# Eight partitions 16 apart instead of 4 apart as the target of each exchange transfer in a gated FFT mix

## The chip, the cores and the metric

The kernel runs on one core of one Trainium2 chip. The metric is the device time of one execution in microseconds. Before the change three executions took 117.07, 117.38 and 120.54 us; the median is 117.38 us.

## What is computed

Two global spectral filters A and B are applied to the same input `x` of 2048 rows by 1024 columns in bf16, and a gate per row mixes them:

```python
X = jnp.fft.rfft2(x.astype(jnp.float32), axes=(-2, -1))
a = jnp.fft.irfft2(X * (A_w_r + 1j * A_w_i), s=(2048, 1024), axes=(-2, -1))
b = jnp.fft.irfft2(X * (B_w_r + 1j * B_w_i), s=(2048, 1024), axes=(-2, -1))
g = sigmoid((x * gate_w).sum(-1, keepdims=True))
out = g * a + (1 - g) * b
```

`A_x` is the `x` of both filters; the weights have 2048 by 513 entries each.

## The kernel before, in words

The row transform of length 2048 is split as 128 times 16. `f1` and `f1j` (L240 to L260) multiply the 16 slabs of x by a constant of 128 columns and leave, for 16 groups `t` of row frequencies, sums in the tile `y`. From there the work is done in 16 units `n`: eight for the even column frequencies (`par` 0) and eight for the odd ones (`par` 1). A unit holds two groups, `t = 2 u + tt` with `u = n % 8` and `tt` 0 or 1. Per unit:

- `f2` (L323) transforms along the columns on TensorE, `tc_` (L336) evicts to bf16 on ScalarE.
- `f3` (L341) does the rest of the row transform, 16 points with twiddles; `xc` (L366) evicts it.
- `cmul` (L382) multiplies by the weights of both filters on VectorE (two instructions, L388). The weights come from HBM, one load of about 0.5 MB per unit, issued on SyncE's queue by `load_w` (L189). Units 0 to 6 are loaded ahead; the later loads are issued inside the unit loop as buffers come free.
- `i1` (L395) adds the products and does the 16-point part of the inverse, for `r` = 0 and 1, 32 matmuls each (L404). `rlc` (L407) evicts each half into the tile `rl`, on ScalarE (L417) or VectorE (L415). `rl` has four buffers (`tag="rl", bufs=4`), so unit n+4 writes the buffer that unit n's transfers read.
- `ex` (L419) is the exchange. It moves `rl` to `RR[par]`, which is the tile `re` for the even units and `ro` for the odd ones, with two DMA transfers issued on GpSimd's queue (L424), one for each `tt`.

The exchange turns the layout around. Row `16 k + s1` of `rl` (k from 0 to 7) belongs to piece k of the group and to slab s1 of the output. A transfer takes the 128 rows of one `tt`, 2 KB each, and writes them to eight partitions, one for each k, in each of them 16 slots of 2 KB, one for each s1. That is 256 KB per transfer, 32 transfers in all. When all eight units of one parity have landed, all 128 partitions of `RR[par]` are filled, and `i2` (L428) contracts over the partitions, slab by slab, with the gated cosines and sines EA and EB as the moving operand. EA and EB are made by `gate_weights` (L312) from the gate and the constant `Ec`, whose row p must hold the wave of the group and piece that lies in partition p; this is the constant "E" (L75). The order of the partitions in `RR` is otherwise free, as `i2` sums over all of them.

After that come the inverse along the columns (`i3e`, `i3q`, `i3o`, `of`), the sums and differences of the halves (`ec`, `eq`, `eg`, `oc`, `fin`), some of them on GpSimd, and eight stores (`st`, and `oc_split` for the last).

The order of all instructions is written out by hand from L577 on. In the loop at L596 the step n holds f2, tc_ of unit n, f3, xc of unit n-1, i1r (i1, rlc and ex) of unit n-3 and the products of unit n-1. The last exchanges are `i1r(14)` and `i1r(15)` (L647, L648). Between them and the first use of `ro`, `op2(0)` at L665, stand the even half's `ep2` and `i3q` work (L649 to L664), which needs only `re`. TensorE takes its work in this order, and what is behind a waiting instruction waits too.

Of the kernel before, what the change touches and what calls it, by code (L numbers as in the profile page):

```python
# [28 lines left out]
def _bf16np(a):  # L29
    return np.ascontiguousarray(np.asarray(a, dtype=np.float32).astype(ml_dtypes.bfloat16))  # L30


def quad_reps(t):
    return (0, 32, 16, 48) if t == 0 else (t, t + 32, t + 64, t + 96)
# [9 lines left out]
def half_rows(t, jh):  # L44
    return np.array([k2 + 128 * k1 for k2 in half_k2(t, jh) for k1 in range(16)])
# [7 lines left out]
def make_constants():  # L53
    c = {}
    s2 = np.arange(128)
    F = np.zeros((128, NT, 2, 2, 2))
    E = np.zeros((NT, 2, 2, 2, 128))
    EZ = np.zeros((NT, 2, 2, 2, 128))
    for t in range(NT):
        for j, k2 in enumerate(quad_reps(t)):  # L60
            th = 2 * np.pi * s2 * k2 / 128
            F[:, t, j // 2, 0, j % 2] = np.cos(th)
            F[:, t, j // 2, 1, j % 2] = -np.sin(th)
            E[t, j // 2, 0, j % 2] = np.cos(th)
            E[t, j // 2, 1, j % 2] = np.sin(th)
            EZ[t, j // 2, 0, j % 2] = 2 * np.cos(th)
            EZ[t, j // 2, 1, j % 2] = -2 * np.sin(th)
            if k2 == 0:
                F[:, t, j // 2, 1, j % 2] = np.cos(np.pi * s2)
                E[t, j // 2, 1, j % 2] = np.cos(np.pi * s2)  # L70
                EZ[t, j // 2, 0, j % 2] = 1
                EZ[t, j // 2, 1, j % 2] = np.cos(np.pi * s2)
    F = F.reshape(128, 128)
    c["F1"] = _bf16np(np.concatenate([F, -F], axis=1))
    c["E"] = _bf16np(E.reshape(2, 4, 2, 8, 128).transpose(2, 0, 3, 1, 4).reshape(128, 128))  # L75
    c["EZ"] = _bf16np(EZ.reshape(128, 128) / 128)
    d = np.arange(256) + 0.5
    i = np.arange(256)
    FD = np.zeros((256, 2, 2, 256))
    dq = DD + 0.5  # L80
    IGE = np.zeros((2, 256, 256))
    IGO = np.zeros((2, 256, 512))
    do = np.concatenate([dq, 512 - dq])
    for eo in range(2):
        m = 2 * i + eo
        FD[:, eo, 0] = np.cos(2 * np.pi * np.outer(d, m) / D)
        if eo == 0:
            IGE[0] = 2 * np.cos(2 * np.pi * np.outer(m, dq) / D)
            IGE[0, 0] = 1
        else:  # L90
            IGO[0] = 2 * np.cos(2 * np.pi * np.outer(m, do) / D)
        m = 2 * i + (2 if eo == 0 else 1)
        FD[:, eo, 1] = -np.sin(2 * np.pi * np.outer(d, m) / D)
        if eo == 0:
            IGE[1] = -2 * np.sin(2 * np.pi * np.outer(m, dq) / D)
            IGE[1, 255] /= 2
        else:
            IGO[1] = -2 * np.sin(2 * np.pi * np.outer(m, do) / D)
    c["FD"] = _bf16np(FD.reshape(2, 128, 2, 2, 256).transpose(1, 2, 3, 0, 4))
    IGE = IGE[:, MSPLIT]  # L100
    c["IGE"] = _bf16np(IGE.reshape(4, 128, 256).transpose(1, 0, 2) / (S * D))
    c["IGO"] = _bf16np(IGO.reshape(4, 128, 512).transpose(1, 0, 2) / (S * D))
    s1 = np.arange(NS1)
    WF = np.zeros((128, NT, 3, 64))
    WI = np.zeros((128, NT, 4, 64))
    for t in range(NT):
        for jh in range(2):
            k = half_rows(t, jh)
            reps = quad_reps(t)[2 * jh:2 * jh + 2]
            al = np.zeros((NS1, 2, 2, 64), dtype=complex)  # L110
            be = np.zeros((2, 2, NS1, 64), dtype=complex)
            for p in range(64):
                w = np.exp(-2j * np.pi * k[p] * s1 / S)
                kk = k[p] % 128
                if kk in (0, 64):
                    cc = 0 if kk == 0 else 1
                    al[:, cc, 0, p] = w
                    be[cc, 0, :, p] = w.conj()
                    continue
                eps = 1 if kk in reps else -1  # L120
                j = reps.index(kk if eps > 0 else 128 - kk)
                al[:, 0, j, p] = w
                al[:, 1, j, p] = 1j * eps * w
                be[0, j, :, p] = w.conj()
                be[1, j, :, p] = 1j * eps * w.conj()
            al = al.reshape(64, 64)
            be = be.reshape(64, 64).T
            h = slice(64 * jh, 64 * jh + 64)
            WF[h, t, 0], WF[h, t, 1], WF[h, t, 2] = al.real, al.imag, -al.imag
            h = h if t % 2 == 0 else slice(64 - 64 * jh, 128 - 64 * jh)  # L130
            WI[h, t, 0], WI[h, t, 1], WI[h, t, 2], WI[h, t, 3] = be.real, be.imag, -be.imag, -be.real
    c["WF"] = _bf16np(WF)
    c["WI"] = _bf16np(WI)
    return c
# [3 lines left out]
def gated_mix(ctx, tc, x_in, we_in, wo_in, gw_in, out):  # L138
    nc = tc.nc
    cn = make_constants()  # L140
    dr = {n: nc.inline_tensor(a, name=f"cst_{n.lower()}").ap() for n, a in cn.items()}
    xv = x_in.flatten_outer_dims()
# [146 lines left out]
    RR = [r[:].rearrange("p (s f) -> p s f", s=NS1) for r in (Re, Ro)]  # L289
# [129 lines left out]
    def ex(n):  # L419
        u, par = n % NU, n // NU  # L420
        rl = RLs.pop(n)
        for tt in range(2):
            p0 = 64 * tt + 32 * (u // 4) + u % 4
            nc.gpsimd.dma_start(RR[par][p0:p0 + 29:4, :, :], rl[:, tt].rearrange("p r m -> p (r m)"))  # L424

    Vs, NV = {}, []

# [73 lines left out]
    def i1r(n, e0, e1):  # L501
        i1(n, 0)
        rlc(n, 0, e0)
        i1(n, 1)
        rlc(n, 1, e1)
        ex(n)
# [245 lines left out]
```

## Time and profile before

| what | us |
|---|---|
| three executions | 117.07, 117.38, 120.54 (median 117.38) |
| the profiled execution, its own time | 117.96 |
| its span | 116.1 |
| TensorE busy | 106.8 (92%) |
| VectorE busy | 95.0 (82%) |
| ScalarE busy | 85.9 (74%) |
| GpSimd busy | 64.5 (56%) |

The profiled execution is 0.58 us above the median; 1.86 us of its time lie outside the span. The mean granted TensorE clock was 0.98. The profile's page gives, for 40 equal slices of the span (2.90 us each), the busy tenths of each engine, the mean busy share of the 16 DMA engines and the GB/s that they moved. The view of groups shows for each line the number of instructions, the mean duration and the idle time of the engine just before them. "To landing" is the time from the issue of a transfer to the last semaphore update that tells of its arrival.

### The profile page before, as it was taken

What the parts mean: (1) busy time and instruction counts of PE and PEld (TensorE: products, weight loads), DVE (VectorE), ACT (ScalarE), POOL (GpSimd) and SP (SyncE); (2) the same over time, 40 slices, a digit from 0 to 9 for tenths busy, and PEclk for the clock granted to TensorE, in tenths of its full rate; (3) what the DMA queues carried; (4) which work ended last, traced back from release to release, by engine and by line L of the source; (5) the groups of instructions that cost most, each with busy time, mean ns of one, the idle gap of its engine ahead of it and who ended that gap; (6) DMA issues with size and microseconds to landing.
All of it is one profiled execution on the core that took longest, in us unless ns stands there. A gap on an engine that the chain in (4) does not pass through costs nothing.

```text
span 116.1 us, 3591 instructions
## 1 busy us (share of the span) xinstructions
PE 106.8 (92%) x1510; PEld 73.3 (63%) x1510; DVE 95.0 (82%) x124; ACT 85.9 (74%) x100; POOL 64.5 (56%) x83
## 2 busy tenths in 40 slices
PE   5999998999999999999999999999997999999900
PEld 2587797855565666555557655659986996677300
DVE  0048799597769999899989999998999779978960
ACT  4078867796998889889899999999756964564300
POOL 1379999902044414244433134446959399999670
PEclk9999999999999999999999999999999999999985
DMA  3999999999999999999999996577840000179684
GB/s 97 329 394 421 363 379 402 418 417 384 397 257 268 228 284 253 287 270 246 251 242 261 270 256 170 147 178 208 211 147 6 0 6 0 51 311 356 251 320 163
DMA packets 11567, 28.73 MB, mean 247 GB/s; under 512 B 3740, under 2 KB 4256, under 8 KB 11552
## 3 DMA queue, kind: packets, MB, share of 16 engines
q1 hardware_dynamic: 6624, 20.02, 47.9%
q0 software_dynamic: 4640, 8.41, 29.4%
q8 instruction: 12, 0.20, 0.7%
q10 hardware_dynamic: 288, 0.07, 0.3%
q14 instruction: 3, 0.02, 0.1%
HBM read 15.89 MB, written 4.19 MB: 173 GB/s over the span
## 4 chain that ended last, share of the span: by engine, by line
PE 51%; POOL 15%; DVE 10%; DMA 9%; issue 6%; ACT 5%; POOLq 1%; ACTq 0%; DVEq 0%
PE pt L404 19%; PE pt L331 9%; PE pt L259 9%; DMA ro<-rl 6%; POOL ot L531 6%; POOL ot L530 6%; DVE y L268 4%; PE pt L354 4%; DMA f<-cst_f 3%; DVE p L388 3%; POOL re L490 2%; DVE rl L415 2%; PE pv L354 2%; PE pv L436 2%; ACT rl L417 2%
## 5 line engine op out<-in xcount | busy, mean ns | idle before, releaser
L404 PE MATMUL pt<-p,wi 64*64 64x512 bf16 x464 | 28.0, 377 | 0.3 <-DVE rl L415 0.3
L388 DVE TENSOR_TENSOR p<-X,w 128x2048 bf16<-128x2048 bf16 (+1 forms) x22 | 25.7, 1224 | 0.1
L404 PEld LDWEIGHTS <-wi 64*64 64x64 bf16 x512 | 15.2, 106 | 9.8 <-issue 0.7
L417 ACT CAST rl<-pt 128x1024 bf16<-128x1024 f32 x21 | 21.4, 1062 | 0.0
L424 POOL DMA_DIRECT2D re<-rl x16 | 9.5, 600 | 19.4 <-issue 5.0
L338 ACT CAST T<-pt 128x1024 bf16<-128x1024 f32 x15 | 15.4, 1026 | 4.1 <-PE pt L331 4.0
L424 POOL DMA_DIRECT2D ro<-rl x16 | 9.5, 598 | 14.1 <-ACT rl L417 9.1
L331 PE MATMUL pt<-fd,y 128*128 128x256 bf16 x120 | 15.9, 274 | 0.6 <-DVE y L268 0.6
L331 PEld LDWEIGHTS <-y 128*128 128x128 bf16 x128 | 11.2, 98 | 7.0 <-issue 4.6
L268 POOL TENSOR_TENSOR y<-ro 128x256 bf16<-128x256 f32 x20 | 13.8, 733 | 0.7 <-ACT ro L285 0.7
L268 DVE TENSOR_TENSOR y<-pt,ro 128x256 bf16<-128x256 f32 x20 | 7.6, 420 | 7.5 <-ACT ro L285 6.9
L376 ACT CAST X<-pt 128x1024 bf16<-128x1024 f32 x12 | 12.6, 1048 | 0.2 <-PE pl L363 0.2
L490 POOL TENSOR_TENSOR re<-w 128x512 f32<-128x512 f32 x8 | 10.2, 1300 | 3.2 <-DVE w L484 1.9
L285 ACT COPY ro<-pt 128x768 f32<-128x768 f32 x10 | 8.0, 799 | 4.3 <-PE pt L259 3.7
L448 ACT CAST V<-pt 128x1024 bf16<-128x1024 f32 x9 | 8.9, 1018 | 2.8 <-PE pt L436 2.8
L415 DVE CAST rl<-pt 128x1024 bf16<-128x1024 f32 x8 | 9.8, 1222 | 1.1 <-PE pt L404 0.9
L259 PE MATMUL pt<-f,re 128*128 128x256 bf16 x80 | 10.5, 295 | 0.1
L259 PEld LDWEIGHTS <-re 128*128 128x128 bf16 x80 | 8.2, 106 | 3.1 <-DMA re<-in_x_dram 1.2
L436 PEld LDWEIGHTS <-ro 128*128 128x128 bf16 x128 | 7.6, 98 | 1.0 <-DMA ro<-rl 0.9
L436 PEld LDWEIGHTS <-re 128*128 128x128 bf16 x128 | 7.4, 98 | 0.7 <-issue 0.4
L354 PE MATMUL pt<-T,wf 64*64 64x512 bf16 (+2 forms) x144 | 7.5, 312 | 0.2 <-ACT T L338 0.2
L354 PEld LDWEIGHTS <-wf 64*64 64x64 bf16 x192 | 4.4, 105 | 5.0 <-issue 3.1
(90 smaller groups left out, 180.5 us busy)
## 6 DMA issues: line engine op xcount, KB each, us to landing
re<-rl POOLq DMA_DIRECT2D x16, 256.0 KB, 8.7
ro<-rl POOLq DMA_DIRECT2D x16, 256.0 KB, 5.5
out_dram<-ot SPq DMA_DIRECT2D x7, 512.0 KB, 3.3
re<-in_x_dram SPq DMA_DIRECT2D x6, 512.0 KB, 7.9
w<-in_wo_dram SPq DMA_DIRECT2D x6, 512.0 KB, 8.0
w<-in_we_dram SPq DMA_DIRECT2D x5, 516.0 KB, 9.0
eab<-in_we_dram SPq DMA_DIRECT2D x3, 516.0 KB, 11.0
re<-in_x_dram SPq DMA_DIRECT2D x4, 256.0 KB, 3.7
```

What stands on the lines that cost most here:

```text
L259: nc.tensor.matmul(o, lhsT=x[:, s1, h * 512 + q * 128:h * 512 + (q + 1) * 128], rhs=(bc(F1[:, 0, :]).to_broadcast([P, 2, 128]) if h == 0 e ...
L268: eng.tensor_tensor(o, i0, i1_, op)
L331: nc.tensor.matmul(ps[:, tt * 512 + r * 256:tt * 512 + r * 256 + 256], lhsT=y[:, par, e, q, 2 * t:2 * t + 2, :, :].rearrange("p j s c -> p ...
L338: nc.scalar.copy(out=T[:].rearrange("p a b -> p (a b)"), in_=PS.pop(("f2", n))[:])
L354: nc.tensor.matmul(ps[ho, tt * 512 + dst:tt * 512 + dst + ln], lhsT=WF[hp(jh), 2 * u + tt, w, :], rhs=T[hp(jh), tt, src:src + ln], start=( ...
L376: nc.scalar.copy(out=xo, in_=ps[:].rearrange("p (t r m) -> p t r m", t=2, r=2))
L388: nc.vector.tensor_tensor(p[:, :, :, 0:M], xb, Ws[n][:, :, :, 0:M], ALU.mult)
L404: nc.tensor.matmul(ps[hp(jh), tt * 512:(tt + 1) * 512], lhsT=WI[hin, 2 * u + tt, w, :], rhs=p[hin, tt, ri::2, o:o + 256], start=(k == 0), ...
L417: nc.scalar.copy(out=o_, in_=i_)
L424: nc.gpsimd.dma_start(RR[par][p0:p0 + 29:4, :, :], rl[:, tt].rearrange("p r m -> p (r m)"))
L436: nc.tensor.matmul(ps[:, s * 512 + ch * 128:s * 512 + ch * 128 + 128], lhsT=RR[par][:, s1, c0 + 256 * ab:c0 + 256 * ab + 128], rhs=Ew[:, s ...
L490: eng.tensor_tensor(o, ls[:, 0], ls[:, 1], op)
```

## The change

Each exchange transfer still writes eight partitions with 16 slots of 2 KB. Before, the partitions were 4 apart, all in one block of 32 partitions: transfer `tt` of unit `u` wrote 64 tt + 32 (u // 4) + u % 4 + 4 k. After, they are 16 apart and lie two in each of the four blocks of 32: it writes 8 tt + u + 16 k. The rows of the constant E follow the new order. Nothing else is changed: sizes, number of transfers, queue, order of issue and buffers stay.

```diff
@@ -72,7 +72,7 @@
     c["F1"] = _bf16np(np.concatenate([F, -F], axis=1))
-    c["E"] = _bf16np(E.reshape(2, 4, 2, 8, 128).transpose(2, 0, 3, 1, 4).reshape(128, 128))
+    c["E"] = _bf16np(E.reshape(8, 2, 8, 128).transpose(2, 1, 0, 3).reshape(128, 128))
@@ -420,8 +420,8 @@
         for tt in range(2):
-            p0 = 64 * tt + 32 * (u // 4) + u % 4
-            nc.gpsimd.dma_start(RR[par][p0:p0 + 29:4, :, :], rl[:, tt].rearrange("p r m -> p (r m)"))
+            p0 = 8 * tt + u
+            nc.gpsimd.dma_start(RR[par][p0:p0 + 113:16, :, :], rl[:, tt].rearrange("p r m -> p (r m)"))
```

## The prediction

> **What bounds the kernel now.** I read the page first: busy shares, slices, queues, chain.
>
> ```profile
> PE   5999998999999999999999999999997999999900
> DMA  3999999999999999999999996577840000179684
> GB/s 97 329 394 421 363 379 402 418 417 384 397 257 268 228 284 253 287 270 246 251 242 261 270 256 170 147 178 208 211 147 6 0 6 0 51 311 356 251 320 163
> q1 hardware_dynamic: 6624, 20.02, 47.9%
> q0 software_dynamic: 4640, 8.41, 29.4%
> PE 51%; POOL 15%; DVE 10%; DMA 9%; issue 6%; ACT 5%; POOLq 1%; ACTq 0%; DVEq 0%
> ```
>
> TensorE is full from the start to about 84 us. The DMA engines are full as well until about 70 us, but from slice 12 (32 us), where the exchanges begin, full engines move about 260 GB/s where they moved up to 421 before. The exchange is q0: 8.41 MB, over a quarter of all engine time.
>
> Next the windows of the two stages of the exchange (columns: window; busy us of PE, PEld, DVE, ACT, POOL; granted clock, DMA share, GB/s), the exchange's line, and its landings in the window 45 to 60 us:
>
> ```profile
> 36.00:70.00 34.00, 33.75 (x560) 20.24 (x556) 32.61 (x34) 31.50 (x35) 11.81 (x20) 1.00 1.01 260
> 70.00:88.00 18.00, 17.42 (x292) 13.07 (x284) 17.52 (x23) 15.80 (x19) 10.96 (x14) 1.00 0.63 166
> ```
>
> ```profile
> re<-rl POOLq DMA_DIRECT2D x16, 256.0 KB, 8.7
> ro<-rl POOLq DMA_DIRECT2D x16, 256.0 KB, 5.5
> ```
>
> ```profile
> L424 POOL DMA_DIRECT2D re<-rl x8: 598/598/598, 46.0 to 57.4; - x8
> DMA to landing us min/median/max: 6.8/9.5/10.5
> ```
>
> With weight loads beside it a transfer takes up to 10.5 us to land; alone, 4 to 5.5 us. Up to 70 us DMA and TensorE are both at their limit.
>
> Last the chain around the end of the exchange (start, us, what), TensorE's timeline there, and two timelines of the eviction and the issue of a unit:
>
> ```profile
> 80.22 0.81 DVE w L484 x2
> 81.03 7.34 DMA ro<-rl
> 88.36 0.05 issue
> 88.41 1.08 PE pv L436 x16
> ```
>
> ```profile
> 86.77 1.03 PE L456 MATMUL pt<-ige,V 128*128 128x256 bf16 x8
> 88.41 1.07 PE L436 MATMUL pv<-eab,ro 128*128 128x128 bf16 x16 [0.61 <-DMA ro<-rl]
> ```
>
> ```profile
> 54.16 1.01 ACT L417 CAST rl<-pt 128x1024 bf16<-128x1024 f32 x1
> ```
>
> ```profile
> 43.18 1.19 POOL L424 DMA_DIRECT2D re<-rl  x2 [2.58 <-ACT T L338]
> ```
>
> The reader should see two places without reserve. First, op2(0) waits for the last transfer: the even half's work covers all but 0.61 us of it, and behind it stands everything to the end (eq(5), GpSimd's eg, the fins, the stores). Second, unit 7 writes the `rl` buffer of unit 3. The second transfer of unit 3 (issued at 43.77) landed at 54.10 by its semaphore updates, 10.33 us after its issue, and unit 7's eviction starts at 54.16. Read the same way for the later units: unit 8 has 1.1 us in hand, 9 has 1.1, 10 has 1.2, 11 has 0.4, 12 has 2.0, 13 has 3.4, 14 has 4.1 and 15 has 0.9. No wait shows today, but a later landing turns into one.
>
> **The change, part by part.**
>
> *The constant E.* Same bytes, other row order: the load (32 KB, landed at 31 us) and the eight gate_weights products on VectorE keep shape and place. Cost nothing.
>
> *Issue on GpSimd.* 598 ns per transfer, 32 times, with the same 8 by 16 pieces of 2 KB. Cost nothing; SyncE's queue is not touched.
>
> *Reading re and ro.* i2 reads all 128 partitions either way (98 ns weight loads). Cost nothing.
>
> *The writes.* Here lies the whole case. The packet records show 64 packets of 4 KB per transfer, written by eight engines at a time in the quiet stretches. Between 70 and 88 us, with no loads about, 73% of the packets take 159 to 175 ns (25.8 GB/s per engine); the others, many at a transfer's start, average 453 ns, all together 239. Between 36 and 70 us the mean is 256 ns, and the load's 4 KB packets take 230 ns there, against 164 ns early in the kernel when loads are alone. The engines handle about 16 packets at any time in both cases, so the stretching is behind the engines: streams that meet on the way into or out of SBUF slow each other.
>
> The change decides which streams meet. Today a transfer's eight streams go to eight places of one 32-block, the two transfers of a unit to different halves. Afterwards each stream has a fellow of the same transfer in the same place of another block, 32 away. No row shows two such streams by themselves, so I bound the price of a packet. Lower end: nothing new is met, 159 ns quiet and 256 mixed; less is excluded as a gain, since TensorE's wait before op2(0) is only 0.61 us (0.9 us with its weight load). Upper end: the fellow adds a full packet to what is met today, 256+159 = 415 mixed and 239+159 = 398 quiet. I take 318 ns (two packets of 159 in turn) for both stages: it is near what a packet that met something already takes in the mixed stage (the slower two thirds average 300 ns), and a stream that is late at a transfer's start leaves the way free for its fellow.
>
> [...]
>
> The sum, landing by landing, as four buffers make unit n+4 wait for unit n:
>
> 1. 36 to 70 us, engines full. 1296 exchange packets start there; 62 ns more each is 80 us of engine time, over 16 engines 5.0 us. The landing of unit 7 (67.84) has 94% of the stage before it: +4.7. The units' reserves (0.06 us at unit 7, 0.4 at unit 11) are too small to take it up, so TensorE, behind the evictions in its order, moves with it.
> 2. Unit 7's landing to unit 11's (76.80): 8.96 us today, with gaps on the engines (share 0.63). Four units are 512 packets; 512 x 318 ns / 16 = 10.2 us: +1.2.
> 3. Unit 11's landing to the last (88.36): 11.56 today. Again 10.2, and the last transfer's slowest engine came 1.3 us after the others: 11.5. No more than today.
>
> Behind op2(0) all moves by the sum, 5.9 us. Against the profiled execution that is 117.96+5.9 = 123.9; this lies 0.58 above the median, so 123.3 for a median.
>
> **The rivals.**
>
> *A. As summed:* 123.3, and with prices from about 287 to 350 ns roughly 119.8 to 128.
>
> *B. Nothing that counts.* If a stream's source, not its target, sets the pace, the new meeting costs nothing. For it: a quiet transfer needs about 2.3 us for eight packets per engine, not 1.3, although its targets are apart today, so something else holds it. Against: most quiet packets run at the engines' full pace, and step 1 needs only 31 ns more per packet to pass 2% (31 x 1296 / 16 x 0.94 = 2.4 us). Time 117.4 to 119.7.
>
> *C. It adds up, and the loads are held too.* [...] With the upper prices: step 1, 159 ns x 1296 / 16 x 0.94 = 12.1; step 2, 512 x 398 / 16 = 12.7, so +3.8; step 3, 12.7+1.3, so +2.5: 18.4 in all, 135.8. For it: the load packets are stretched today by exchange writes (230 against 164 ns). Against: two stretches that overlap do not add. [...]
>
> *D. Faster.* After the change the exchange leaves half of the places at any time to the loads. If load packets went back from 230 to 164 ns, 841 of them would free 3.5 us of the stage. It decides only where something waits for the DMA: TensorE is busy 33.75 of 34 us there, and after 80 us it waits 0.61 to 0.9 us for the exchange. Hence at best 116.5, inside 2%.
>
> **How the numbers follow.** A 0.62, B 0.14, C 0.22, D 0.02. I predict the time of A, 123.3 us. The 2% bound (about what a measurement of this kernel can tell from no change) is 119.7. A and C are slower: 0.84. B and a D within the bound are the same: 0.15; faster 0.01. The range starts at 119.0, which leaves out most of B and D (0.13), and goes to 133.0, well into C, leaving out its upper part (0.07).
>
> **What would show it.** If A is right: the exchange's quiet packets are near 318 ns instead of 159; q0's share rises from 29.4% to about 35% of a span of 122 us; ScalarE's or VectorE's evictions to `rl` (L417, L415) show waits for re<-rl or ro<-rl, from about unit 7 on; TensorE is no longer full between 54 and 84 us; the last landing is near 94 us and the stretch behind op2(0) keeps its length. If B is right, the packets and the landings are those of before. If C is right, L198's loads land later too (9.0 us median in the window 36 to 62 now), and the first rl waits come before unit 7. I am wrong in the sum if the wait for `rl` shows but the exchange catches up after 70 us, or if the packets stretch and nothing waits.

## The result, and the profile after

The changed kernel takes 124.44 us (median of six executions, 123.88 to 125.42). Against the kernel before on the same chips the ratio is 1.058, with a 95% interval of 1.049 to 1.067: slower by nearly 7 us. The ratios below are of undisturbed executions alone, as some others were longer (the kernel before took up to 121.36 us) and the profiles of the runs with six buffers and with eight neighbours show a lower granted clock in part. The profiled execution of the changed kernel took 124.58 us with a span of 122.7 us.

The page of the changed kernel (TensorE and DMA by slices; queues with packets, MB and share of engine time; chain by engine and by line):

```profile
PE   6999998999999973998996959999995999999900
DMA  2999999999989999999999999899992000087684
q1 hardware_dynamic: 6624, 20.02, 47.2%
q0 software_dynamic: 4640, 8.41, 35.6%
PE 25%; DMA 24%; POOL 15%; DVE 13%; ACT 11%; issue 8%; POOLq 1%; ACTq 0%; DVEq 0%
```

TensorE has holes between the slices 15 and 24 (42.9 to 73.6 us), where it was full before, and the DMA engines are now full to about 92 us, not 70. The exchange's share of engine time rose from 29.4% to 35.6% for the same bytes and packets. On the chain TensorE fell from 51% to 25% and DMA rose from 9% to 24%.

The windows of the two stages, and the exchange's median time to landing:

```profile
36.00:70.00 34.00, 29.49 (x474) 17.69 (x467) 26.69 (x27) 25.87 (x28) 9.70 (x17) 1.00 1.04 217
70.00:88.00 18.00, 16.42 (x287) 11.17 (x286) 16.88 (x21) 17.18 (x19) 7.48 (x13) 1.00 0.97 191
```

```profile
re<-rl POOLq DMA_DIRECT2D x16, 256.0 KB, 13.8
ro<-rl POOLq DMA_DIRECT2D x16, 256.0 KB, 8.1
```

In the first stage full engines move 217 GB/s instead of 260, and TensorE lacks 4.5 of 34 us. Landings of the even half went from 8.7 to 13.8 us, those of the odd half from 5.5 to 8.1.

By the packet records an exchange packet (4 KB) takes 318 ns on average between 70 and 88 us (median 306.5; before 239 and 159), and only 12% stay at 175 ns or less (before 73%). Between 36 and 70 us the mean is 328 ns (before 256). Load packets there went from 230 to 280 ns.

Who waits, by the view of waits (total us, times, longest):

```profile
ACT rl L417 <- DMA re<-rl: 4.1, 4, 1.4
...
DVE rl L415 <- DMA re<-rl: 4.0, 2, 2.3
...
PE pl L363 <- issue: 2.7, 1, 2.7
```

The first two lines did not exist before: evictions now wait for the transfer that reads their buffer. ScalarE's timeline has the second of them, unit 7's; unit 3's transfers, issued at 42.35, landed at 57.04:

```profile
57.10 1.01 ACT L417 CAST rl<-pt 128x1024 bf16<-128x1024 f32 x1 [0.87 <-DMA re<-rl]
```

The third line is another thing, a stop of TensorE in the middle of a group of matmuls; the last run and the last section are about it.

The landings by their semaphore updates: unit 7 at 73.90 us (before 67.84), unit 11 at 83.90 (76.80), the last at 95.01 (88.36). Behind the last there are 27.7 us of span before and after, so the whole 6.6 us of span arose ahead of it. The changed kernel's profile had a small head start: its first exchange transfer was issued at 31.54 us, 0.8 us sooner than before (32.36). Over all profiles here this issue lies between 31.3 and 33.6 us, whatever the layout, so the head start is not put down to the change. Counted from the first issue, unit 7's landing came 6.9 us later than before, not 6.1.

### The profile page after: what moved, and what is told of

It reads as the page before. It is cut to its first block, busy times and chain, and to the rows that moved or that the text cites. A ratio compares the mean times of both kernels' runs of the same rounds, so it can differ in the third digit from the quotient of the medians.

```text
span 122.7 us, 3589 instructions
## 1 busy us (share of the span) xinstructions
PE 106.9 (87%) x1508; PEld 73.6 (60%) x1510; DVE 95.1 (78%) x124; ACT 86.2 (70%) x100; POOL 64.3 (52%) x83
## 3 DMA queue, kind: packets, MB, share of 16 engines
q0 software_dynamic: 4640, 8.41, 35.6%
## 4 chain that ended last, share of the span: by engine, by line
PE 25%; DMA 24%; POOL 15%; DVE 13%; ACT 11%; issue 8%; POOLq 1%; ACTq 0%; DVEq 0%
DMA re<-rl 24%; PE pt L259 8%; ACT rl L417 7%; POOL ot L531 5%; POOL ot L530 5%; DVE y L268 4%; PE pt L331 4%; PE pt L404 4%; DVE w L484 3%; PE pt L354 2%; PE pt L169 2%; POOL re L490 2%; PE pt L298 1%; DVE p L388 1%; ACT T L338 1%
## 5 line engine op out<-in xcount | busy, mean ns | idle before, releaser
L404 PE MATMUL pt<-p,wi 64*64 64x512 bf16 x464 | 28.5, 377 | 1.1 <-issue 0.6
L417 ACT CAST rl<-pt 128x1024 bf16<-128x1024 f32 x21 | 21.3, 1067 | 6.5 <-DMA re<-rl 4.1
L404 PEld LDWEIGHTS <-wi 64*64 64x64 bf16 x512 | 15.8, 106 | 10.5 <-issue 2.1
L331 PEld LDWEIGHTS <-y 128*128 128x128 bf16 x128 | 11.1, 98 | 7.8 <-issue 5.4
L415 DVE CAST rl<-pt 128x1024 bf16<-128x1024 f32 x8 | 9.8, 1221 | 6.3 <-DMA re<-rl 4.0
L268 POOL TENSOR_TENSOR y<-ro 128x256 bf16<-128x256 f32 x20 | 13.8, 740 | 0.3 <-ACT ro L285 0.3
L490 POOL TENSOR_TENSOR re<-w 128x512 f32<-128x512 f32 x8 | 10.2, 1295 | 4.0 <-DVE w L484 2.6
L259 PE MATMUL pt<-f,re 128*128 128x256 bf16 x80 | 9.9, 282 | 0.0
## 6 DMA issues: line engine op xcount, KB each, us to landing
re<-rl POOLq DMA_DIRECT2D x16, 256.0 KB, 13.8
```

What stands on the lines that cost most here:

```text
L259: nc.tensor.matmul(o, lhsT=x[:, s1, h * 512 + q * 128:h * 512 + (q + 1) * 128], rhs=(bc(F1[:, 0, :]).to_broadcast([P, 2, 128]) if h == 0 e ...
L268: eng.tensor_tensor(o, i0, i1_, op)
L331: nc.tensor.matmul(ps[:, tt * 512 + r * 256:tt * 512 + r * 256 + 256], lhsT=y[:, par, e, q, 2 * t:2 * t + 2, :, :].rearrange("p j s c -> p ...
L404: nc.tensor.matmul(ps[hp(jh), tt * 512:(tt + 1) * 512], lhsT=WI[hin, 2 * u + tt, w, :], rhs=p[hin, tt, ri::2, o:o + 256], start=(k == 0), ...
L417: nc.scalar.copy(out=o_, in_=i_)
L490: eng.tensor_tensor(o, ls[:, 0], ls[:, 1], op)
```

## The experiments

Each run is compared with the kernel before, run on the same chip. Unless said otherwise the short diffs are against the changed kernel, and E's rows follow the new order. A "way" is what two writing streams share when they slow each other; "quiet" packets are the exchange's 4 KB packets between 70 and 88 us, when no loads are about. The letters P, W, B, D and F in the expectations stand for theories named there; B and D are not the prediction's rivals B and D.

### Two transfers that meet

```diff
-            p0 = 8 * tt + u                     # step 16
+            p0 = 32 * (u // 2) + 2 * (u % 2) + tt
+            nc.gpsimd.dma_start(RR[par][p0:p0 + 29:4, :, :], ...)
```

> Each transfer keeps eight partitions 4 apart in one block of 32, but the two transfers of a unit now go to the same block (32 (u // 2) + 2 (u % 2) + tt + 4 k), so they meet in the same eight groups of four partitions. Theory P (a way into SBUF belongs to a group of four partitions together with the group 32 away; two streams on one way halve each other, whichever transfer they come from): exchange packets near 318 ns when no loads are about, as after the change, and 123 to 125.5 us. Rival W (only the streams of one transfer hinder each other): packets near 159 ns, 117 to 119 us.

Ratio 1.056 (1.042 to 1.069), the loss of the change itself. Quiet packets have a median of 301 ns and a mean of 308. A layout with steps of 4, as before, loses as much if the two transfers of a unit are aimed at the same groups. Theory P holds, W falls.

### Steps of 8

```diff
-            p0 = 8 * tt + u                     # step 16
+            p0 = 64 * tt + u
+            nc.gpsimd.dma_start(RR[par][p0:p0 + 57:8, :, :], ...)
```

> Each transfer writes eight partitions 8 apart inside one half of 64 (64 tt + u + 8 k): two blocks instead of four, but again four pairs that lie 32 apart. Theory P: as after the change, 123 to 126 us, quiet packets near 318 ns. Rival D (spread over blocks): about half of the loss, 119.5 to 122 us.

Ratio 1.071 (1.064 to 1.078); quiet median 312 ns. Half the spread, the full loss: the pairs 32 apart count, not the number of blocks.

### Steps of 12, twice

```diff
+            t = 2 * u + tt
+            p0, sp = (t, 12) if t < 12 else (84 + t, 4)
+            nc.gpsimd.dma_start(RR[par][p0:p0 + 7 * sp + 1:sp, :, :], ...)
```

> Twelve of the sixteen transfers of a parity write eight partitions 12 apart, which lie in three blocks of 32, each in a group of four of its own (no two of them 32 or less than 4 apart); the other four write 4 apart in the last block. Theory P: nothing is shared inside a transfer, so close to before: 117 to 120 us, most quiet packets near 159 ns (the two transfers of a unit, one partition apart, can meet, which may cost up to the same as the change: a result up to 125 would then show packets near 318 ns only while both are under way). Rival D (it is the spread over several blocks that is slow): as after the change, 123 to 126 us, with quiet packets near 318 ns at all times.

Ratio 1.066 (1.048 to 1.084), quiet median 304 ns. It did not separate the theories: nothing coincides inside a transfer, but the second transfer of a unit lies one partition beside the first and so meets it everywhere, as the expectation allowed. The placement was mended:

```diff
+    if u < 4:
+        return (u, 12) if tt == 0 else (96 + u, 4)
+    return (u + 4 * tt, 12)
```

> Steps of 12 again (three blocks of 32), but the two transfers of a unit are placed so that only two of their sixteen groups of four coincide: units 0 to 3 of a parity write u + 12 k and 96 + u + 4 k, units 4 to 7 write u + 12 k and u + 4 + 12 k. Theory P: close to before, most quiet packets near 159 ns again, 117 to 120.5 us. Rival D (the spread over several blocks is slow as such): 123 to 126 us with quiet packets near 310 ns, as for the run with steps of 12 before.

Ratio 1.018 (1.009 to 1.027), a third of the loss. Its windows:

```profile
36.00:70.00 34.00, 32.36 (x528) 19.69 (x524) 30.36 (x31) 29.52 (x32) 11.43 (x20) 1.00 1.03 235
70.00:88.00 18.00, 17.54 (x301) 12.87 (x294) 17.54 (x22) 16.52 (x20) 9.04 (x13) 1.00 0.91 205
```

The same steps over three blocks as in the run before it, and TensorE has 32.36 of 34 us where the change left 29.49. The spread as such (D) is out as the cause of the loss. The quiet packets came down only to a median of 233 ns, 34% at 175 or less, not to 159 as expected: counted by theory P's groups, two in sixteen still coincide inside a unit, and a unit's first transfer shares two or three of its eight groups with the second of the unit before, where it shared none before the change. That this is the whole rest was not tried.

### Eight neighbours

```diff
-            p0 = 8 * tt + u                     # step 16
+            p0 = 16 * u + 8 * tt
+            nc.gpsimd.dma_start(RR[par][p0:p0 + 8, :, :], ...)
```

> Each transfer writes eight neighbouring partitions (16 u + 8 tt + k), so four streams share each of two groups of four. Theory P: a way gives about 26 GB/s whatever comes, so a quiet packet takes about 4 x 159 = 636 ns, a unit's exchange 5.1 us instead of TensorE's 3.3, and the sixteen units take some 80 us from 33 us on: 140 to 152 us. Rival (only partitions 32 apart hinder each other): 117 to 119 us.

Ratio 1.329 (1.312 to 1.347), from two executions of 155.25 and 156.97 us. The window after the loads are through, where units 8 to 15 land 4.7 us apart:

```profile
88.00:130.00 42.00, 29.89 (x384) 21.18 (x376) 24.17 (x29) 21.38 (x25) 14.81 (x18) 0.83 1.04 108
```

Full engines move 108 GB/s; packets have a median of 593 ns, 3.7 times the 159 ns of a packet that meets nothing. That is near four packets in turn, as two groups of four neighbours would give. So neighbours share (a median of 593 ns here) as well as partitions 32 apart (312 with steps of 8). The time was expected at 140 to 152 us and came out longer: I had put no loads into it, and with loads about units 0 to 7 land 7.0 us apart instead of 5.1. That the loads explain all of it was not tried.

Where two streams meet, the medians here are 301 to 312 ns and the means 308 to 324; where four meet, the median is 593 and the mean 608. My 318 lies among the means of two.

### Which half of the exchange costs

```diff
+            p0, sp = (8 * tt + u, 16) if par == 0 else (64 * tt + 32 * (u // 4) + u % 4, 4)
```

> The changed order for the eight even units only; the odd units write 4 apart as before, while the constant follows the new order, so the odd half of the product gets the wrong rows of the wave (timing is unaffected). Theory: nearly all of the loss arises up to unit 7's landing, with loads about, and TensorE is full behind it, so it isn't won back: 121.5 to 124 us. Rival (the last landings make the loss): 117.5 to 119.5 us.

The other run has `par == 1` in that line.

> The changed order for the eight odd units only, the even ones 4 apart as before (again with the wrong rows of the wave for one half). Theory: little load traffic is left, 2.5 us of writing per unit fits TensorE's pace of about 3 us, and only the last landing comes later: 118 to 120.5 us. Rival (the last landings make the loss): 122 to 124 us.

Even half alone: 1.049 (1.039 to 1.059). Odd half alone: 1.010 (1.001 to 1.020). The two add up to the loss of the change. The first stage of the even run, then of the odd one:

```profile
36.00:70.00 34.00, 29.63 (x472) 17.93 (x465) 27.11 (x28) 26.28 (x29) 9.46 (x17) 1.00 1.05 224
```

```profile
36.00:70.00 34.00, 33.77 (x560) 20.23 (x553) 32.63 (x34) 31.16 (x35) 11.04 (x19) 1.00 1.03 245
```

With the even units on shared ways TensorE is busy 4.1 us less there than before the change (33.75) and is behind for good. With the odd ones it loses nothing there. Later, evictions wait 1.8 us in all for ro<-rl, and TensorE's wait ahead of op2(0) grows only from 0.6 to 1.2 us, though quiet packets take 335 ns on average.

### Without the loads

The nine loads of units 7 to 15 are left out; those units use weights that are in SBUF already.

```diff
-        nc.sync.dma_start(w, w_in[par][u])
+        if n < 7:
+            nc.sync.dma_start(w, w_in[par][u])
```

> The changed kernel without the nine weight loads of units 7 to 15: those units multiply by weights that lie in SBUF already (other numbers, same shapes). Theory: the exchange alone, 2.5 to 2.6 us of writing per unit, fits TensorE's pace of 3.3 us until unit 11; quiet packets stay near 318 ns, but no eviction waits for re<-rl and TensorE is full to 80 us: 117.5 to 120 us. Rival (the exchange on shared ways is the bound by itself): 122 to 125 us, with the waits still there.

> The kernel before the change without the same nine loads, as the other side of the last run. Theory: TensorE is the bound there, so about as before, 116 to 118 us; the exchange's landings fall from 8.7 us (even half) to about 5. Rival (the full DMA engines cost time before the change as well): 112 to 115 us.

Ratios to the kernel before: 1.004 (0.999 to 1.010) with the change, 0.996 (0.990 to 1.001) without it, medians 117.90 and 116.85 us. Of nearly 7 us about 1 is left. The windows with the change, and the first window without it:

```profile
36.00:70.00 34.00, 33.76 (x564) 20.24 (x560) 32.62 (x35) 31.46 (x34) 11.42 (x20) 1.00 0.73 157
70.00:88.00 18.00, 17.15 (x288) 12.92 (x280) 17.52 (x22) 15.78 (x20) 11.17 (x15) 1.00 0.78 159
```

```profile
36.00:70.00 34.00, 33.76 (x564) 20.18 (x560) 32.61 (x34) 31.46 (x35) 11.09 (x19) 1.00 0.62 156
```

The exchange on shared ways occupies 73% of the engines, TensorE is full, and no eviction waits, though packets still average 295 ns in the first window and 307 in the second. The even half lands in 5.7 us instead of 13.8 (without the change in 4.8 instead of 8.7, about 5 as expected). What is left is at the end, in the view of waits:

```profile
PE pv L432 <- DMA ro<-rl: 1.2, 1, 1.2
```

So neither the exchange nor the loads are too much by themselves; the change takes the slack that the two together had left. Before the change the loads cost next to nothing: without them that kernel gains 0.5%, with an interval that just takes in no gain.

### More buffers

Units 7, 8, 11 and 12 are evicted to a free part of `y`.

```diff
+            if n in (7, 8, 11, 12):
+                k = 4096 + 2048 * ((n - 7) % 4)
+                RLs[n] = y[:, 0].rearrange("p e q t s c -> p (e q t s c)")[:, k:k + 2048].rearrange("p (t r m) -> p t r m", t=2, r=2)
```

> The changed kernel, with units 7, 8, 11 and 12 evicted to a part of y that is free by then, so that from unit 7 on six buffers stand behind the exchange instead of four. Theory P with the DMA engines as the bound: the waits of the evictions for re<-rl go, but the exchange is no faster; last landing 95.0 within 1 us, 123 to 125 us. Rival B (the four buffers are the bound): TensorE runs ahead by the 3 to 4 us that it now waits, the last landing comes near 92 us, and the time is 121 to 122 us.

Ratio 1.060 (1.048 to 1.073): no gain. The first stage:

```profile
36.00:70.00 34.00, 31.65 (x516) 18.82 (x512) 29.95 (x31) 29.26 (x32) 10.53 (x18) 1.00 1.04 215
```

TensorE does get more done there, 31.65 us instead of 29.49, but the DMA engines are full at 215 GB/s, the changed kernel's rate, and the last landing is at 95.5 (at a granted clock of 0.93 between 70 and 94 us). The time is the one expected with the engines as the bound, but the run is no clean test. The waits of the evictions, which were to go, only moved: they are 6.5 us for re<-y, where units 11 and 12 write again what units 7 and 8 use, and 0.6 us for re<-rl. GpSimd too now waits before it issues (4.6 us for re<-rl in the view of waits), so not all of the room was used. That the engines are the bound in the first stage is better shown by the run without the loads, where no eviction waits.

### TensorE's stops

```diff
-    for _ in range(6):
+    for _ in range(2):
```

> The changed kernel with two instead of six warming matmuls at the start, which takes eight instructions out of TensorE's stream. After the change TensorE stops three times, at its recorded instructions 1217, 1473 and 1729, 256 apart, each time about 3 us after a 16 KB transfer of the instruction queue starts. Theory F (it waits for its own instructions, whose transfers queue on the same full DMA engines): the stops come at the same counts from the start, 1217, 1473, 1729, that is eight instructions later in the program. Rival (it waits for data at these places): at the same matmuls as before, that is at counts 1209, 1465, 1721. No change of time beyond 1 us.

One execution, 124.75 us. Of the three stops only the first is there, and it is at the same count, 1217. The waits for data moved with the program: 1728, 1848, 2485 and 2568 where they were at 1736, 1856, 2493 and 2576. The stop at 1217 was inside the last matmuls of f3 (L363) and is now behind the first matmul of i1 (16 matmuls for each `r`, 32 for a unit):

```profile
48.13 1.93 PE L404 MATMUL pt<-p,wi 64*64 64x512 bf16 x31 [0.51 <-issue]
```

For that stop the count of theory F came and not the rival's 1209: it belongs to a place in the instruction stream, not to a matmul. What TensorE waits for there is not shown by it. For 1473 and 1729 this run says nothing, but the others do: stops that wait for nothing the profile shows come at 1217 also with two transfers that meet, steps of 8, six buffers, the even half alone and eight neighbours (4.0 us there), at 1473 with steps of 8, six buffers and the mended steps of 12, and at 1729 with two transfers that meet and six buffers.

## Why the prediction was right, point by point

- *The ways.* The price of a packet was put at 318 ns from bounds of 159 and 398 in the quiet stage; it measured 318 on average. In the mixed stage 318 was taken and 328 measured. That the mean came out to the nanosecond is partly luck: half of the quiet packets took 306.5 ns or less, 12% no more than 175, and longer ones make up for it. The sharing itself, which no row of before showed, is now shown by the runs with steps of 4 (a quiet median of 301 ns), 8 (312) and 1 (593), against 159 before.
- *Step 1, to unit 7's landing.* Predicted +4.7 us, measured +6.1, or +6.9 from the first issue on. This term was too small. It kept the loads' packets at 230 ns and left their slowing to rival C; they took 280, and 841 of them at 50 ns more, over 16 engines and with the 0.94, are 2.5 us of engine time; the exchange's own 72 ns instead of 62 add 0.8. Together that would be 8.0, more than was seen, so the terms do not simply add.
- *Step 2, to unit 11.* Predicted +1.2 (10.2 us for four units), measured 10.0 us, +1.0. The engines were full there (share 0.97), as said.
- *Step 3, to the last landing.* Predicted 11.5 us and no more than before; measured 11.1, which gives 0.45 back. (The prediction's "alone, 4 to 5.5 us" leaves out the last transfer, which took 7.3 us to land, and 8.0 after the change.)
- *The sum.* Predicted 5.9 us against the profiled execution, measured 6.6 (124.58 against 117.96); for the median 123.3 was predicted and 124.44 measured. Part of that closeness is luck: without the head start of 0.8 us the two profiles would be some 7.4 us apart, if it carried through to the end. The mechanism, the path and the place of the loss were right, and behind op2(0) nothing changed, as predicted.
- *The signs.* q0's share at 35.6% (about 35 was said), the last landing at 95.0 (near 94), waits for re<-rl at L417 and L415, TensorE not full. One came sooner: the first such wait is unit 6's, not unit 7's, and unit 5 is already late by TensorE's stop at 48.00.
- *The free edits.* E's rows, the issue on GpSimd (592 ns each now) and the reads by i2 (98 ns weight loads) cost nothing.
- *The rivals.* B would have needed quiet packets as before. Both signs that were set for C came: loads land later (median 11.0 us instead of 9.0 in the stage), and the first wait for `rl` is ahead of unit 7. So what C named, loads that are held up too, is there beside A, but small: C's upper prices, 18.4 us in all, did not come. Whether a load packet is slow because its engine stands behind a slow write, or because it meets exchange streams on its own way, no run separates. D's premise is refuted: load packets got slower, from 230 to 280 ns, not faster.

## What to carry to other kernels

A transfer's cost is not in its bytes and packets alone: with the same ones, a quiet packet of 4 KB had a median of 159 ns before, 301 to 312 in the layouts where two streams meet and 593 where four do. Look at which partitions the streams under way at the same time write, across transfers too. In the layouts tried here, those to keep apart were streams to a common group of four neighbours or to its fellow 32 further on. Whether such a loss counts is read from the stage: here it was nearly 7 us where the DMA engines were full beside a full TensorE, and about 1 us once either the loads or the even half's sharing was gone. Before moving a transfer, compare the landing of each buffer's last reader with the start of its next writer; a reserve of 0.06 us is a wait in the making.

## What the runs showed of the hardware that was not expected

TensorE stopped three times in the changed kernel where the profile shows nothing that it waited for. Queue 8, of the kind "instruction" on the page, moves 12 packets of 16 KB (0.7% of engine time), which is one for every 254 of the 3045 records of TensorE and its weight loads and queue. In the changed kernel's timeline, inside one group of eight matmuls:

```profile
45.15 0.20 PE L363 MATMUL pl<-T,wf 64*64 64x1 bf16 x5
48.00 0.20 PE L363 MATMUL pl<-T,wf 64*64 64x1 bf16 x3 [2.65 <-issue]
```

```profile
56.66 0.85 PE L404 MATMUL pt<-p,wi 64*64 64x512 bf16 x11 [0.59 <-issue]
```

```profile
65.70 0.50 PE L331 MATMUL pv<-fd,y 128*128 128x256 bf16 x3 [0.56 <-issue]
```

Counted in TensorE's records the three stops lie at 1217, 1473 and 1729, exactly 256 apart, and each ends 2.8 to 3.2 us after a 16 KB packet of queue 8 begins (44.90, 53.43, 62.92). Before the change there is no such stop at these counts. They sum to 3.8 us, but they are not 3.8 us of the loss: in the run with two warming matmuls only 0.5 us of such stops is left, and the time was 124.75 us all the same (one execution).

Full engines alone do not make the stop, as they were full before the change as well (share 1.01). What differs is how far ahead of TensorE the packet begins. I pair the fourth packet with count 1217, as the stop there follows it. It begins 6.0 us before TensorE gets there in the changed kernel without the loads and 4.0 us ahead in the kernel before, with no stop in either. With the change it begins only 0.45 us ahead (stop of 2.65 us), with steps of 8 it is 1.5 us ahead (1.65 us), and with eight neighbours 1.4 us late (4.0 us). In all seven runs that stop at 1217 the stop ends 2.7 to 3.1 us after that packet begins, which looks as if TensorE waits for what is left of about 3 us from that packet's start. This is my estimate from these times: no record names what ended the stops. Why the packet begins late was not tried.
